# Transposed gating with gates spread by a broadcast load, over lighter query and key DMA, in a fused attention and mixture-of-adapters kernel

## The chip, the cores and the metric

The kernel runs on one core of one Trainium2 chip (trn2). The metric is device time in microseconds (us) of that core, the median of the runs. "Span" is the time from the first to the last instruction of the one profiled execution; a run's time lies about 2 us above its span. A run counts as slow when it lies over 1.5% above the fastest run of the same kernel; comparisons use the others, called fast.

## The reference, cut to what matters

```python
def _attn_ref(q, kv, w_sr):            # q: 4 x 12288 x 128; kv: 4 x 384 x 32 x 128
    kv_pool = kv.reshape(B, H // 4, 4, W // 4, 4, C).mean(axis=(2, 4))
    k = v = kv_pool.reshape(B, -1, C) @ w_sr          # 768 keys a batch
    a = softmax((q @ k.transpose(0, 2, 1)) / sqrt(C))
    return a @ v

def _moe_ref(x, w_gate, A, B):         # x: 49152 x 128; 8 experts of rank 16
    logits = x @ w_gate
    topk = top two experts of each row; w = softmax of their two logits
    delta[row] = sum over the two e of  w_e * ((x[row] @ A[e]) @ B[e])
    return x + delta
```

(The two functions are shortened here to the formulas; `softmax` and `top two` stand for their lines.) The adapters' part, delta, is small beside x. The comparison with the reference doesn't tell right gates from wrong ones.

## The kernel before

The queries are cut into 96 chunks of 512, 24 to a batch; four chunks make a group. The loop is a software pipeline, its instructions kept in program order (`keep`). At step k, TensorE computes the scores of chunk k, the attention sums of an earlier one, and the adapters of still earlier ones.

```python
    def mm(*a, **k):
        return keep(nc.tensor.matmul(*a, **k))        # every matmul has this line: L68
    # ...
    def cast_q(g):                                    # fp32 -> bf16, DRAM to DRAM, issued by GpSimd
        t = qdram.tile([GT, C], BF16, tag=f"q{g}", name=f"qbf{g}")
        keep(nc.gpsimd.dma_start(t, q[g // NG, (g % NG) * GT:(g % NG + 1) * GT]))
        q_bf[g] = t

    def load_qT(g):
        t = qpool.tile([P, GT], BF16, tag="qT", name="qT")
        keep(nc.sync.dma_start(t.rearrange("c (j p) -> c j p", p=P),
                               q_bf[g].rearrange("(p j) c -> p (j c)", p=P), transpose=True))
        qT[g] = t
    # ...
    def scores(k, r):                                 # r = 0, 1, 2: two of six key tiles each
        # ...
        ps = ps_s.tile([P, 2, T], FP32, tag="sg", name="sg")       # two buffers
        for i in range(2):
            mm(ps[:, i], kfT[b][:, 2 * r + i], rhs, start=True, stop=True)
        keep(nc.scalar.activation(em[k][:, 2 * r:2 * r + 2], ps, AF.Exp, bias=0.0, scale=scale))
    # ...
    def gates(k0, n, eng, arg, mask):                 # one call a group, eng is GpSimd
        th = rpool.tile([P, GC * S, 8], FP32, tag="th", name="th")[:, 0:n]
        keep(nc.scalar.activation(th, arg, AF.Tanh, bias=0.0, scale=0.5))
        w = gpool.tile([P, GC * S, 8], FP32, tag="gw", name="gw")
        keep(eng.tensor_tensor(w[:, 0:n], th, mask, op=ALU.mult))
        keep(eng.tensor_tensor(w[:, 0:n], w[:, 0:n], mask, op=ALU.add))
        gw[k0] = w
    # transposes(kx, kh): x of chunk kx and gated h of chunk kh, on TensorE into one PSUM tile
    # of two buffers (tt_ps, pool ps_m), then copied out by VectorE (tts)
    def down(k):
        hp[k] = mtile([P, S, P], name="h_ps")
        for s in range(S):
            mm(hp[k][:, s], xT[k][:, s], a_bf, start=(s == 0), stop=(s == S - 1))

    def gate(k):
        # ...
        keep(nc.vector.tensor_tensor(hg[k] ..., hp[k] ..., gw[k0] ... broadcast over the rank, op=ALU.mult))

    def up(k):
        dp[k] = mtile([P, S, C], name="d_ps")
        for s in range(S):
            mm(dp[k][:, s], hgT[k][:, s], b_bf, start=(s == 0), stop=(s == S - 1))
    # ... when a chunk's x may enter the adapters, in steps:
        done = normed[first[k] + size[k] - 1]         # the group's last chunk is normalized
        late = k < NCHUNK - 2
        # ...
        e = max(e if two else e + 1, done + late)
    # ... in the loop over steps k:
        if k % GC == 0:
            g = k // GC
            if 2 <= g + 1 < B * NG:
                load_qT(g + 1)
            if 4 <= g + 2 < B * NG and g + 2 not in q_bf:
                cast_q(g + 2)
        if b + 1 < B:
            if i == 4:
                sums, rest = prepare(b + 1, nc.gpsimd)    # pooling additions of the next keys
            if 4 <= i < 16:
                h, j = divmod(i - 4, 4)
                load_kv(b + 1, h, j, None)                # 512 KB each
```

The softmax here doesn't subtract the row's maximum and nothing guards it: scores larger than these inputs give would overflow.

## Time and profile before

| | before |
|---|---|
| time, median of 3 fast runs | 426.5 us (426.18 to 426.99) |
| span of the profiled run | 423.3 us |
| start, to the first exp of chunk 4 | 31.5 us |
| chunks 4 to 95, first exp to first exp | 364.2 us |
| tail, after the first exp of chunk 95 | 27.6 us |
| usual period of one chunk | 3.68 us |

The periods are worked out from the trace as the difference between the starts of the first exp of successive chunks.

The page of the kernel before: busy time, share of the span and instruction count of each engine; busy tenths in 40 equal slices for TensorE (PE) and for the DMA engines; DMA packets, MB and share of 16 engines by queue; the chain that ended last, by engine; and three groups of instructions, with busy time, mean nanoseconds of one, and idle time ahead of them with the releaser of most of it.

```profile
span 423.3 us, 11396 instructions
PE 389.1 (92%) x4589; PEld 308.8 (73%) x4589; DVE 327.3 (77%) x967; ACT 292.8 (69%) x336; POOL 162.5 (38%) x263
PE   4898999999999999999999999999999999999853
DMA  8989557776556998765647999998575628342112
q1 hardware_dynamic: 70128, 64.11, 52.7%
q0 software_dynamic: 704, 11.54, 14.5%
PE 72%; DVE 10%; POOL 8%; ACT 3%; DMA 2%; issue 2%; SPq 1%; ACTq 0%; DVEq 0%
...
L246 ACT ACTIVATE em<-sg 128x1024 f16<-128x1024 f32 x288 | 280.5, 1023 | 97.3 <-PE sg L68 96.4
...
L350 DVE TENSOR_TENSOR hg<-h_ps,gw 128x512 bf16<-128x512 f32 x96 | 66.1, 688 | 29.9 <-POOL gw L315 16.1
...
L68 PE MATMUL tt_ps<-id_bf,hg 128*128 128x128 bf16 x384 | 38.1, 223 | 3.2 <-DVE hg L350 2.8
```

TensorE is full in nearly every slice and makes up 72% of the chain; DMA makes up 2%, although its engines are well used (52.7% and 14.5% of the 16 engines' time in the two main queues). The last two groups are what the change is aimed at: VectorE waits 16.1 us for gates that GpSimd (POOL) has late, and 384 matmuls transpose the gated h.

The table of windows of the kernel before, in a stretch without key preparation and over a longer one: the window, its length, busy time of PE, PEld, DVE, ACT and POOL with instruction counts, granted TensorE clock, DMA share, GB/s.

```profile
205.90:238.20 32.30, 32.30 (x407) 26.15 (x406) 27.99 (x79) 24.90 (x28) 8.14 (x17) 1.00 0.72 184
200.00:270.00 70.00, 68.50 (x849) 55.05 (x846) 58.35 (x169) 53.72 (x61) 31.92 (x48) 1.00 0.84 204
```

PE is busy 32.30 of 32.30 us: here only fewer or shorter matmuls make a chunk shorter.

The timeline of the kernel before around one late gate (start, length, engine, line, operation; in brackets the idle time before it and its releaser):

```profile
57.05 0.54 PE L68 MATMUL acc<-vx,em 128*128 128x137 f16 x6
57.42 0.59 PE L68 MATMUL sg<-qT,kfT 128*128 128x512 bf16 x2
...
60.24 2.49 POOL L171 TENSOR_TENSOR kvr<-kvr 128x512 f32<-128x512 f32 x2
...
63.23 0.45 POOL L315 TENSOR_TENSOR gw<-gw,over 128x128 f32<-128x128 f32 x1
63.71 0.69 DVE L350 TENSOR_TENSOR hg<-h_ps,gw 128x512 bf16<-128x512 f32 x1 [1.82 <-POOL gw L315]
```

Two pooling additions hold POOL for 2.49 us, the gates come behind them, and VectorE stands 1.82 us.

### The profile page before, as it was taken

What the parts mean: (1) busy time and instruction counts of PE and PEld (TensorE: products, weight loads), DVE (VectorE), ACT (ScalarE), POOL (GpSimd) and SP (SyncE); (2) the same over time, 40 slices, a digit from 0 to 9 for tenths busy, and PEclk for the clock granted to TensorE, in tenths of its full rate; (3) what the DMA queues carried; (4) which work ended last, traced back from release to release, by engine and by line L of the source; (5) the groups of instructions that cost most, each with busy time, mean ns of one, the idle gap of its engine ahead of it and who ended that gap; (6) DMA issues with size and microseconds to landing.
All of it is one profiled execution on the core that took longest, in us unless ns stands there. A gap on an engine that the chain in (4) does not pass through costs nothing.

```text
span 423.3 us, 11396 instructions
## 1 busy us (share of the span) xinstructions
PE 389.1 (92%) x4589; PEld 308.8 (73%) x4589; DVE 327.3 (77%) x967; ACT 292.8 (69%) x336; POOL 162.5 (38%) x263
## 2 busy tenths in 40 slices
PE   4898999999999999999999999999999999999853
PEld 3566777787877878787888778777888877788642
DVE  2644678788988878779888878779888888888853
ACT  3478567686777777676788777676777866678522
POOL 0010357965320557964330467963231312222000
PEclk9999999999999999999999999999999999999965
DMA  8989557776556998765647999998575628342112
GB/s 302 397 214 284 110 182 199 276 161 140 128 123 134 335 252 258 286 159 114 158 126 150 318 248 164 355 135 182 130 170 129 150 76 175 108 119 75 52 63 88
DMA packets 71172, 76.43 MB, mean 181 GB/s; under 512 B 49904, under 2 KB 50160, under 8 KB 70640
## 3 DMA queue, kind: packets, MB, share of 16 engines
q1 hardware_dynamic: 70128, 64.11, 52.7%
q0 software_dynamic: 704, 11.54, 14.5%
q8 instruction: 36, 0.59, 0.6%
q14 instruction: 16, 0.13, 0.1%
q10 hardware_dynamic: 288, 0.07, 0.1%
HBM read 50.53 MB, written 36.70 MB: 206 GB/s over the span
## 4 chain that ended last, share of the span: by engine, by line
PE 72%; DVE 10%; POOL 8%; ACT 3%; DMA 2%; issue 2%; SPq 1%; ACTq 0%; DVEq 0%
PE acc L68 28%; PE sg L68 23%; PE tt_ps L68 9%; PE d_ps L68 5%; PE h_ps L68 4%; POOL kvr L171 4%; DVE hg L350 3%; ACT em L246 2%; DVE osb L363 2%; DVE xn L263 2%; POOL over L293 1%; PE v_ps L68 1%; SPq L98 1%; PE kpT_ps L68 1%; DMA kvr<-in_kv_dram 1%
## 5 line engine op out<-in xcount | busy, mean ns | idle before, releaser
L246 ACT ACTIVATE em<-sg 128x1024 f16<-128x1024 f32 x288 | 280.5, 1023 | 97.3 <-PE sg L68 96.4
L68 PE MATMUL acc<-vx,em 128*128 128x137 f16 x2304 | 174.1, 224 | 2.0 <-DVE xn L263 1.9
L68 PE MATMUL sg<-qT,kfT 128*128 128x512 bf16 x576 | 170.9, 378 | 2.7 <-ACT em L246 2.2
L68 PEld LDWEIGHTS <-em 128*128 128x128 f16 x2304 | 149.8, 98 | 4.9 <-DVE xn L263 2.2
L68 PEld LDWEIGHTS <-tts 128*128 128x128 bf16 x768 | 59.1, 99 | 53.0 <-ACT tts L334 5.6
L350 DVE TENSOR_TENSOR hg<-h_ps,gw 128x512 bf16<-128x512 f32 x96 | 66.1, 688 | 29.9 <-POOL gw L315 16.1
L293 POOL TENSOR_TENSOR over<-xn,srt 128x128 f32<-128x128 f32 (+1 forms) x54 | 19.8, 384 | 175.7 <-DVE srt L281 175.7
L263 DVE TENSOR_TENSOR xn<-acc,rinv 128x544 f32<-128x544 f32 x96 | 69.5, 724 | 3.3
L171 POOL TENSOR_TENSOR kvr<-kvr 128x512 f32<-128x512 f32 x54 | 67.4, 1268 | 2.1 <-DMA kvr<-in_kv_dram 1.9
L363 DVE TENSOR_TENSOR osb<-d_ps,xn 128x512 f32<-128x512 f32 x96 | 65.9, 689 | 2.7 <-PE d_ps L68 2.6
L336 DVE COPY tts<-tt_ps 128x1024 bf16<-128x1024 bf16 (+1 forms) x95 | 63.9, 672 | 2.4 <-PE tt_ps L68 2.4
L68 PEld LDWEIGHTS <-xn 128*128 128x128 bf16 x384 | 29.5, 99 | 28.6 <-issue 6.1
L68 PEld LDWEIGHTS <-kfT 128*128 128x128 bf16 x576 | 45.9, 97 | 6.0 <-issue 3.7
L68 PE MATMUL h_ps<-a_bf,tts 128*128 128x128 bf16 x384 | 37.6, 221 | 6.1 <-ACT tts L334 3.9
L68 PE MATMUL tt_ps<-id_bf,xn 128*128 128x128 bf16 x384 | 37.5, 221 | 6.0 <-DVE hg L350 4.4
L258 DVE RECIPROCAL rinv<-acc 128x4 f32<-128x4 f32 x96 | 17.3, 180 | 32.9 <-PE acc L68 32.2
L68 PE MATMUL tt_ps<-id_bf,hg 128*128 128x128 bf16 x384 | 38.1, 223 | 3.2 <-DVE hg L350 2.8
L68 PE MATMUL d_ps<-b_bf,tts 128*128 128x128 bf16 x384 | 38.0, 224 | 2.6 <-DVE hg L350 1.0
L281 DVE MAX8 srt<-xn 128x8 f32<-128x8 f32 x384 | 34.5, 153 | 0.2
L68 PEld LDWEIGHTS <-hg 128*128 128x128 bf16 x384 | 26.1, 100 | 4.2 <-DVE hg L350 3.7
L312 ACT ACTIVATE th<-over 128x128 f32<-128x128 f32 (+2 forms) x33 | 9.1, 276 | 15.5 <-DVE over L298 12.2
L314 POOL TENSOR_TENSOR gw<-th,over 128x128 f32<-128x128 f32 (+1 forms) x27 | 11.0, 406 | 21.6 <-ACT th L312 21.5
(49 smaller groups left out, 162.4 us busy)
## 6 DMA issues: line engine op xcount, KB each, us to landing
out_dram<-osb SPq DMA_DIRECT2D x96, 256.0 KB, 3.3
kvr<-in_kv_dram SPq DMA_DIRECT2D x36, 512.0 KB, 6.2
qbf<-in_q_dram POOLq DMA_DIRECT2D x22, 512.0 KB, 6.7
kvr<-in_kv_dram SPq DMA_DIRECT2D x24, 256.0 KB, 4.9
qf<-in_q_dram SPq DMA_DIRECT2D x1, 1024.0 KB, 5.1
qf<-in_q_dram SPq DMA_DIRECT2D x4, 256.0 KB, 5.1
qT<-qbf SPq DMA_TRANSPOSE x22, 8.1
w_sr_sb<-in_w_sr_dram ACTq DMA_DIRECT2D x1, 64.0 KB, 4.7
```

What stands on the lines that cost most here:

```text
L68: return keep(nc.tensor.matmul(*a, **k))
L171: keep(adder.tensor_tensor(u[:, lo:hi], u[:, lo:hi], v[:, lo:hi], op=ALU.add))
L246: keep(nc.scalar.activation(em[k][:, 2 * r:2 * r + 2], ps, AF.Exp, bias=0.0, scale=scale))
L258: keep(nc.vector.reciprocal(ri, acc[k][:, :, VC]))
L263: keep(nc.vector.tensor_tensor(x, acc[k][:, :, 0:VC], ri.unsqueeze(2).broadcast_to([P, S, VC]), op=ALU.mult))
L281: keep(nc.vector.max(srt[k0][:, m, s], xn[k][:, s, C:VC]))
L293: keep(eng.tensor_tensor(d, lg, so[:, :, i].unsqueeze(2).broadcast_to([P, n, 8]), op=ALU.subtract))
L312: keep(nc.scalar.activation(th, arg, AF.Tanh, bias=0.0, scale=0.5))
L314: keep(eng.tensor_tensor(w[:, 0:n], th, mask, op=ALU.mult))
L336: keep(nc.vector.tensor_copy(sb[:, lo:hi], ps[:, lo:hi]))
L350: keep(nc.vector.tensor_tensor(hg[k].rearrange("p s (e r) -> p (s e) r", e=E), hp[k].rearrange("p s (e r) -> p (s e) r", e=E), gw[k0][:, m ...
L363: keep(nc.vector.tensor_tensor(osb, dp[k], xn[k][:, :, 0:C], op=ALU.add))
```

## The change

Intent: for 84 of the 96 chunks, compute h already transposed (one matmul of 512 columns), so that its transpose goes. The gates must then lie along the columns and be the same for the 16 rank rows of an expert. They are transposed once per group on TensorE, written to DRAM (32 KB), and read back 16-fold (512 KB); this trip gets five steps instead of one. Under it, the DMA is rearranged: the query transposes read 16 rows instead of 128 and come two groups ahead, the key loads are cut to 256 KB and spread evenly.

```diff
     def load_qT(g):
         t = qpool.tile([P, GT], BF16, tag="qT", name="qT")
-        keep(nc.sync.dma_start(t.rearrange("c (j p) -> c j p", p=P),
-                               q_bf[g].rearrange("(p j) c -> p (j c)", p=P), transpose=True))
+        keep(nc.sync.dma_start(t.rearrange("c (j r) -> c j r", r=16),
+                               q_bf[g].rearrange("(r j) c -> r (j c)", r=16), transpose=True))
# ... scores: exp now reads PSUM with a step of 64 elements (from group 2 on)
+        if k // GC > 1:
+            ps = ps.rearrange("p i (j s r) -> p i s r j", s=S, r=16)
+            o = o.rearrange("p i (s r j) -> p i s r j", s=S, r=16)
# ... after the tanh of the gates
+        if k0 in turned:                  # chunks 4 to 87: 18 groups of four, 6 of two
+            # ... gh[k0]: the gates in fp16, made on GpSimd
+            turns.append([lambda: turn_gates(k0, n), lambda: spread_gates(k0, n)])
+            return
+    def turn_gates(k0, n):                # one step later
+        ps = mtile([P, P], FP16, name="gT_ps")
+        mm(ps[0:n * E], gh[k0][:, 0:n * E], id_h, is_transpose=True, start=True, stop=True)
+        sb = gtpool.tile([P, P], FP16, tag="gT", name="gT")
+        keep(nc.vector.tensor_copy(sb[0:n * E], ps[0:n * E]))
+        gt[k0] = gdram.tile([P, P], FP16, tag="gt", name="gt")
+        keep(nc.sync.dma_start(gt[k0][0:n * E], sb[0:n * E]))
+
+    def spread_gates(k0, n):              # again one step later
+        gx[k0] = gxpool.tile([P, GT], FP16, tag="gx", name="gx")
+        src = gt[k0][0:n * E].rearrange("(e s) t -> e (s t)", e=E)
+        keep(nc.sync.dma_start(gx[k0][:, 0:n * P],
+                               src.unsqueeze(0).broadcast_to([RK, E, n * P])))
     def down(k):
         hp[k] = mtile([P, S, P], name="h_ps")
+        if first[k] in turned:
+            mm(hp[k], a_bf, xT[k], start=True, stop=True)
+            return
# ... gate: hgT = hp * gx for these chunks; rows of A and B reordered to fit
-        late = k < NCHUNK - 2
+        late = TURN if first[k] in turned else k < NCHUNK - 2      # TURN = 5
# ... other pairs of chunks share a step at the end
+        if k % GC == 0 and 5 <= g + 3 < B * NG:
+            cast_q(g + 3)
+        while nload < min(24 * (B - 1), k + 8, 2 * (k - LA) + 2):   # one 256 KB key load a step
+            bn, n = divmod(nload, 24)
+            load_kv(bn + 1, n // 8, n % 8 // 2, n % 2)
+            nload += 1
+        if k % GC == 1 and 2 <= g + 1 + (g > 1) < B * NG:
+            load_qT(g + 1 + (g > 1))
# ... pools: qpool 4 to 3, ppool 7 to 6, xpool 5 to 6; B loaded in 8 pieces at the start
```

## The prediction

> **What bounds it now.** TensorE. The page gives PE 389.1 of 423.3 us, full granted clock except at the ends. Starts of each chunk's first score matmul, read from the trace: most of 91 periods are 3.68 us; in the stretch 205.9 to 238.2 us the table of windows has PE busy 32.30 of 32.30 us, VectorE 27.99, ScalarE 24.90. That is pure matmul streaming. By the timeline starts lie 0.22 us apart per four 128-column matmuls, 1.12 us per 18 of 137, so: scores about 1.29, attention 1.50, four small groups (x transpose, down, h transpose, up) 0.22 each.
>
> The periods over 3.68 add up to 29 us. About 6 us per later batch are in steps with key preparation. Some 2.7 of these are its own matmuls (timeline); 3.3 are mostly gates late on POOL behind 1.27 us pooling additions (63.2 us: VectorE idle 1.82 us for POOL; the table of waits sums 16.1 us of this). That is about 10 us of the span.
>
> **What the change does.** Of 96 chunks, 84 are gated transposed.
> - PE: the h transpose goes (0.22 us a chunk) and down becomes one 512-column matmul (same time). Added: one 128-column transpose per group, 24 times 0.06. Net -0.22 x 84 + 1.3, about -18 us, all on the critical path; the period becomes about 3.45 us.
> - VectorE: the transpose copy shrinks from 0.69 to 0.42 us (table of groups): about 3.0 us per 3.45.
> - Gates enter the pipeline five steps after normalization instead of one, so lateness on POOL is absorbed: -8 of the 10 us.
> - New DMA chain per group: write gates to DRAM (stores land in 3.3 us), read back 16-fold, 512 KB (loads land in 5 to 6 us). The code leaves some 9.4 us from issue to use, about 1 us of slack: I allow 3 us of waits.
> - Tail: more chunks are unfinished when the scores end (the schedule ends two steps later) (last 24 us: PE busy 10.55). +5 us.
> - Query transposes: 45,056 packets of 256 B, 26 ns each, 74 us of 16 engines; DMA is almost absent from the waits, so lighter or smoother DMA gains little.
> - ScalarE: exp now reads PSUM with a step of 64 elements. Three of 1023 ns per chunk, 2.9 us. [...]this trace has no such read. I take no change. If wrong, ScalarE becomes the bound: at 1.2 us a piece the period is 3.6 and the gain half gone; at twice the time the kernel is far slower.
>
> **Sum.** 423.3 - 18 - 8 + 5 + 3 = 405 us of span; runs lie 2 to 3 us above it: 407 us, 80% range 399 to 420. Faster by over 2% 0.80, within 2% 0.12, slower 0.08.
>
> **What would show it.** Clean periods 3.45 us, PE gapless there; exp mean near 1023 ns; no wait of the gate product for POOL, few for the gate load; steps with key preparation at most 0.6 us over the others; the tail after the last score matmul about 5 us longer; h transposes only for 12 chunks.
>
> **What would make it wrong.** Strided exp slower than 1.15 us; gate loads landing late and blocking VectorE[...]; 16-row query transposes heavier instead of lighter, holding up the SP queue; the tail growing by 10 us or more.

That exp takes no longer with a step of 64 elements was my assumption; no run had shown it then.

## The result, and the profile after

The kernel became slower: 445.75 us, median of 4 runs (444.31 to 449.79), against 426.75 for the kernel before (four runs, one of them slow, 438.66). The ratio is 1.0465, 95% interval 1.0375 to 1.0556. Ratios here are the mean time of one kernel's fast runs over that of the other's of the same rounds, so they are not quite the ratio of the quoted medians.

The page of the kernel after, the same parts, and the DMA issues of the gates (count, KB each, median us from issue to landing):

```profile
span 442.8 us, 10496 instructions
PE 387.9 (88%) x4025; PEld 288.1 (65%) x4025; DVE 308.8 (70%) x987; ACT 297.9 (67%) x341; POOL 163.8 (37%) x263
PE   4897989899989977899899999979999999997464
DMA  8997679999899796878999898899667855433023
q1 hardware_dynamic: 37248, 75.81, 60.5%
q0 software_dynamic: 704, 11.54, 14.8%
PE 48%; DMA 28%; DVE 11%; POOL 5%; issue 3%; ACT 2%; SPq 2%; DVEq 0%; ACTq 0%
...
L256 ACT ACTIVATE em<-sg 128x1024 f16<-128x1024 f32 x288 | 281.6, 1023 | 103.4 <-PE sg L71 102.4
...
L386 DVE TENSOR_TENSOR hgT<-h_ps,gx 128x512 bf16<-128x512 f32 x84 | 58.1, 691 | 35.6 <-DMA gx<-gt 22.6
...
gx<-gt SPq DMA_DIRECT2D x18, 512.0 KB, 5.4
...
gt<-gT SPq DMA_DIRECT2D x18, 32.0 KB, 4.1
```

The 564 matmuls are gone (4,589 to 4,025) and exp costs what it did, 1023 ns, in spite of its step of 64 elements. But PE's row has 7s now, and DMA went from 2% to 28% of the chain. The gate product no longer waits for POOL; it waits 22.6 us for the gates' read-back, gx. (PE's busy time fell by only 1.2 us. A busy PE is not one at full clock: below it is busy 3.00 of 3.00 us at a clock of 0.62. The mean granted clock fell from 0.979 to 0.961; no run splits this number further.) The casts' queue, q0, carries the same 704 packets; the main queue has half the packets, as the query transposes became lighter, but more bytes and a larger share, 60.5% after 52.7%, as the gates' trip came to it.

The timeline of the kernel after, one late read-back link by link:

```profile
162.72 0.58 POOL L82 DMA_DIRECT2D qbf<-in_q_dram  x1
163.22 0.58 SPq L342 DMA_DIRECT2D gt<-gT  x1
...
168.24 0.54 PE L71 MATMUL acc<-vx,em 128*128 128x137 f16 x6
168.70 0.59 PE L71 MATMUL sg<-qT,kfT 128*128 128x512 bf16 x2
...
172.31 0.52 SPq L347 DMA_DIRECT2D gx<-gt  x1
...
177.32 0.69 DVE L386 TENSOR_TENSOR hgT<-h_ps,gx 128x512 bf16<-128x512 f32 x1 [4.38 <-DMA gx<-gt]
...
178.07 0.38 PE L71 MATMUL tt_ps<-id_bf,xn 128*128 128x128 bf16 x4 [3.26 <-DVE hgT L386]
...
179.58 0.38 PE L71 MATMUL d_ps<-b_bf,hgT 128*128 128x128 bf16 x4 [0.53 <-DVE tts L368]
```

A cast of a query group (qbf) leaves at 162.72, the store of the gates (gt) 0.5 us after it. The read-back (gx) needs that store and can't leave before 172.31. It takes its usual 5.0 us, and VectorE stands 4.38 us and PE 3.26 us behind it. VectorE took nothing out of order here: a reciprocal further on in its program (rinv), whose matmuls had ended at 174.37, started at 178.26, after the gate product. Here the store was late, not the load. The table of waits of the kernel after, first by engine (in all, times, longest) and then for SyncE's queue, has the whole run:

```profile
DVE hgT L386 <- DMA gx<-gt: 22.6, 11, 4.4
```

```profile
SPq L347 <- DMA gt<-gT: 41.2, 20, 5.3
```

SyncE must see the store landed before it can send the read-back; it stands 41.2 us in 20 for that. But not all of the eleven waits have a late store. By the landings in the trace, three of them (10.8 of the 22.6 us) came behind a store of over 7 us, two (3.5 us) behind a read-back of over 7 us, and six (8.3 us) behind a store of at most 5.0 and a read-back of at most 6.2 us. In those six the store left late. The timeline of the kernel after ahead of one of them (VectorE's copy of the gates, then SyncE's issues):

```profile
144.21 0.21 DVE L340 COPY gT<-gT_ps 128x128 f16<-128x128 f16 x1
...
144.46 3.54 SPq L410 DMA_DIRECT2D out_dram<-osb  x1
148.05 2.60 SPq L101 DMA_DIRECT2D kvr<-in_kv_dram  x1
150.75 0.54 SPq L342 DMA_DIRECT2D gt<-gT  x1
```

VectorE has written the gates at 144.42. SyncE is then at an output store and a key load, for 3.54 and 2.60 us, and sends the gates behind them, 6.3 us later: it issued in program order and not in the order of what was ready; VectorE waits 2.87 us for them in the end. In the six the store left 1.3 to 6.3 us after the copy.

The chain that ended last, of the kernel after, shows a late store again (start, length, what):

```profile
278.07 7.36 DMA gt<-gT
...
285.49 5.34 DMA gx<-gt
290.93 0.70 DVE hgT L386
```

The 32 KB store takes 7.36 us of the chain and the 512 KB load 5.34.

The table of windows of the kernel after, over the stretch shown of before, in the stall above, and right after it:

```profile
200.00:270.00 70.00, 66.50 (x730) 49.60 (x728) 54.72 (x174) 52.89 (x59) 27.09 (x44) 1.00 0.92 240
...
174.00:181.00 7.00, 3.21 (x27) 2.06 (x25) 3.27 (x11) 2.25 (x3) 6.74 (x8) 0.92 0.92 269
181.00:184.00 3.00, 3.00 (x25) 2.55 (x24) 1.50 (x4) 1.02 (x1) 1.51 (x2) 0.62 1.17 206
```

The DMA share rose from 0.84 to 0.92. In the stall PE is busy 3.21 of 7 us, and in the 3 us after it the granted clock is 0.62. The clock is 0.50 from 179.84 to 183.25 us, after this gap of 3.26 us, and again from 292.5 to 295.9 us, after a gap of 2.63 us. At 180.45 two score matmuls take 1.06 us, at 178.46 and 184.04 they take 0.59. This stall so cost more than its own length: the chunk with it has a period of 9.83 us, where the same chunk without the trip (e3 below) has 4.38.

From the starts of each chunk's first exp, the spans split as follows (us):

| kernel | to the first exp of chunk 9 | chunks 9 to 83 | from chunk 84 to the end | span |
|---|---|---|---|---|
| before | 56.2 | 296.5 | 70.7 | 423.3 |
| after | 58.2 | 299.0 | 85.7 | 442.8 |

So there are two questions. Why did chunks 9 to 83, which lost a matmul group each, not get shorter? And why is the end 15 us longer?

A hint at the first is in the landings. The 24 gate stores took 5.5 us (median) when a cast or a query transpose was in flight for 1.4 us or more of that time, and 3.1 us when for less (at most 0.4 us). The five longest, 6.2 to 9.5 us, all had a cast in flight for 6.0 to 8.4 us of that time. The DMA engines were not busier then (0.72 to 0.92 of the 16 engines) than around the short landings on both sides of 230 us (0.92 to 0.94). A long store has more time to meet a cast, so this alone proves nothing; e11 and e12 test it.

### The profile page after: what moved, and what is told of

It reads as the page before. It is cut to its first block, busy times and chain, and to the rows that moved or that the text cites. A ratio compares the mean times of both kernels' runs of the same rounds, so it can differ in the third digit from the quotient of the medians.

```text
span 442.8 us, 10496 instructions
## 1 busy us (share of the span) xinstructions
PE 387.9 (88%) x4025; PEld 288.1 (65%) x4025; DVE 308.8 (70%) x987; ACT 297.9 (67%) x341; POOL 163.8 (37%) x263
## 3 DMA queue, kind: packets, MB, share of 16 engines
q1 hardware_dynamic: 37248, 75.81, 60.5%
## 4 chain that ended last, share of the span: by engine, by line
PE 48%; DMA 28%; DVE 11%; POOL 5%; issue 3%; ACT 2%; SPq 2%; DVEq 0%; ACTq 0%
PE acc L71 19%; PE sg L71 16%; DMA gx<-gt 9%; DMA gt<-gT 8%; DMA kvr<-in_kv_dram 7%; PE d_ps L71 4%; PE h_ps L71 4%; PE tt_ps L71 4%; POOL kvr L177 2%; DMA a_f<-in_moe_A_dram 2%; DVE hgT L386 2%; DVE tts L368 2%; DVE osb L403 2%; DVE xn L273 2%; ACT tts L366 2%
## 5 line engine op out<-in xcount | busy, mean ns | idle before, releaser
L256 ACT ACTIVATE em<-sg 128x1024 f16<-128x1024 f32 x288 | 281.6, 1023 | 103.4 <-PE sg L71 102.4
L71 PEld LDWEIGHTS <-em 128*128 128x128 f16 x2304 | 153.5, 99 | 21.7 <-DVE xn L273 5.0
L386 DVE TENSOR_TENSOR hgT<-h_ps,gx 128x512 bf16<-128x512 f32 x84 | 58.1, 691 | 35.6 <-DMA gx<-gt 22.6
L71 PEld LDWEIGHTS <-kfT 128*128 128x128 bf16 x576 | 48.1, 98 | 16.9 <-issue 9.8
L71 PEld LDWEIGHTS <-hgT 128*128 128x128 bf16 x336 | 25.6, 98 | 30.0 <-issue 13.4
L268 DVE RECIPROCAL rinv<-acc 128x4 f32<-128x4 f32 x96 | 17.4, 181 | 37.2 <-PE acc L71 37.1
L368 DVE COPY tts<-tt_ps 128x512 bf16<-128x512 bf16 (+1 forms) x90 | 38.2, 424 | 2.0 <-PE tt_ps L71 2.0
L71 PE MATMUL d_ps<-b_bf,hgT 128*128 128x128 bf16 x336 | 32.3, 220 | 7.5 <-DVE tts L368 7.1
L71 PE MATMUL h_ps<-tts,a_bf 128*128 128x512 bf16 x84 | 32.2, 384 | 2.5 <-DVE tts L368 2.5
L323 ACT ACTIVATE th<-over 128x128 f32<-128x128 f32 (+2 forms) x33 | 9.0, 274 | 14.4 <-DVE over L309 11.0
L175 POOL TENSOR_TENSOR kvr<-kvr 128x512 f32<-128x512 f32 (+1 forms) x18 | 18.0, 998 | 1.4
L71 PEld LDWEIGHTS <-tts 128*128 128x128 bf16 x96 | 8.1, 118 | 15.0 <-ACT tts L366 11.8
L366 ACT COPY tts<-tt_ps 128x1024 bf16<-128x1024 bf16 (+1 forms) x10 | 8.0, 796 | 14.7 <-PE tt_ps L71 14.7
```

The costliest lines, as they stand in the source:

```text
L175: keep(adder.tensor_tensor(u, u, v, op=ALU.add))
L256: keep(nc.scalar.activation(o, ps, AF.Exp, bias=0.0, scale=scale))
L268: keep(nc.vector.reciprocal(ri, acc[k][:, :, VC]))
L366: keep(nc.scalar.copy(sb[:, lo:hi], ps[:, lo:hi]))
L368: keep(nc.vector.tensor_copy(sb[:, lo:hi], ps[:, lo:hi]))
L386: keep(nc.vector.tensor_tensor(hgT[k], hp[k], gx[k0][:, m * T:(m + 1) * T].rearrange("p (s t) -> p s t", s=S), op=ALU.mult))
```

## The experiments

The quoted expectations name some theories by letters and say there what each means; the text around them uses words. The table gives each kernel's time, and the same three stretches of its profiled run. Slow runs are in the medians and ranges and not in the ratios, so the ratios of e2, e15 and e16 rest on two fast runs each. One run of the kernel before took 668.27 us, at a clock of 0.562; it counts as slow.

| run | median (range), us | before | ratio of fast runs, 95% interval | to chunk 9 | 9 to 83 | 84 to end |
|---|---|---|---|---|---|---|
| e1 | 426.55 (426.14–427.21) | 426.71 | 1.0001 [0.9982, 1.0020] | 56.3 | 296.6 | 71.4 |
| e2 | 451.75 (444.85–455.28) | 426.71 | 1.0471 [1.0408, 1.0533] | profile of a slow run | | |
| e3 | 425.35 (425.16–425.59) | 426.71 | 0.9971 [0.9956, 0.9987] | 58.8 | 279.4 | 85.5 |
| e4 | 434.94 (433.79–438.75) | 426.71 | 1.0224 [1.0161, 1.0287] | 59.4 | 288.3 | 84.1 |
| e5 | 434.9 (433.84–436.44) | 426.57 | 1.0190 [1.0158, 1.0222] | 59.0 | 288.0 | 87.7 |
| e6 | 451.99 (448.25–466.53) | 426.57 | 1.0558 [1.0509, 1.0607] | 60.9 | 302.2 | 87.1 |
| e7 | 438.37 (435.40–440.17) | 426.57 | 1.0261 [1.0211, 1.0312] | 58.1 | 294.0 | 83.2 |
| e8 | 431.86 (431.31–433.95) | 426.57 | 1.0125 [1.0090, 1.0161] | 58.5 | 283.8 | 88.0 |
| e9 | 429.85 (425.16–435.82) | 426.66 | 1.0075 [1.0048, 1.0102] | 58.2 | 279.4 | 85.7 |
| e10 | 440.15 (436.43–444.12) | 426.66 | 1.0287 [1.0233, 1.0341] | 59.4 | 294.5 | 85.4 |
| e11 | 425.68 (424.99–427.92) | 426.66 | 0.9986 [0.9954, 1.0018] | 59.3 | 279.3 | 84.3 |
| e12 | 434.06 (431.94–435.35) | 426.66 | 1.0169 [1.0132, 1.0205] | 59.2 | 286.2 | 85.6 |
| e13 | 427.48 (421.90–432.41) | 426.91 | 0.9955 [0.9916, 0.9994] | profile of a slow run | | |
| e14 | 426.86 (422.43–433.03) | 426.91 | 0.9955 [0.9916, 0.9994] | profile of a slow run | | |
| e15 | 436.61 (431.98–444.64) | 426.91 | 1.0135 [1.0115, 1.0156] | 60.7 | 286.0 | 84.3 |
| e16 | 442.80 (434.44–448.08) | 427.02 | 1.0213 [1.0124, 1.0302] | 63.6 | 282.7 | 86.4 |
| e17 | 460.34 (458.77–461.50) | 427.02 | 1.0759 [1.0706, 1.0812] | 63.5 | 308.9 | 85.9 |
| e18 | 421.02 (419.38–421.78) | 426.10 | 0.9865 [0.9826, 0.9903] | 57.8 | 276.3 | 84.6 |

### e1_dma_only and e2_gating_only: the two halves apart

e1 is the kernel before with the DMA half alone: 16-row query transposes two groups ahead, the strided exp and the permuted store that follow from them, and 256 KB key loads at one pace. e2 is the kernel after with that half undone. Neither changes the other half's lines.

```diff
 # e1, against the kernel before
+        keep(nc.sync.dma_start(t.rearrange("c (j r) -> c j r", r=16), ..., transpose=True))
+            ps = ps.rearrange("p i (j s r) -> p i s r j", s=S, r=16)      # in scores
+        while nload < min(24 * (B - 1), k + 8, 2 * (k - LA) + 2): ...     # key loads
+        if k % GC == 1 ...: load_qT(g + 1 + (g > 1))
```

> Only the DMA half of the change (16-row query transposes two groups ahead, the permuted exp and store, key loads of 256 KB at one pace), with the old gating. Theory W (the loss in the main part is the new gates' trip through DRAM arriving late at VectorE): no gate load here, so about the time before, 418 to 428 us. Rival D (the new pattern of DMA is itself the loss): 435 us or more, with waits for keys or queries.

> Only the gating half, over the old DMA (128-row transposes one group ahead, key loads in bursts of 512 KB). Theory W: the gate loads are as late or later, so 440 to 460 us, with the gate product waiting 20 us or more for the gate load. Rival D: 405 to 420 us, since the DMA pattern is gone.

The DMA half alone changed nothing: ratio 1.0001, and each stretch within 0.7 us of the kernel before. The gating half alone carried the whole loss, 1.0471 against 1.0465 for both. (Its profile is of a slow run, so it is no measure; the gate product waits 33.4 us for the read-back in it.) The query transposes did get lighter: by the packets in the trace, 45,056 of 256 B, 74.3 us of 16 engines' time, became 352 of 32 KB, 52.1 us. Their median landings were 8.1 us in the kernel before and 6.6 in the kernel after, counted from where SyncE reaches the instruction, so with its waits for a free buffer. That relief was on nothing that ended a wait.

### e3_no_gate_dma and e4_traffic_no_wait: the trip's wait, or its traffic

Both multiply h by a constant, so no instruction waits for the read-back (the result is wrong). e4 still sends both DMAs; e3 sends neither.

```diff
 # e4, against the kernel after
+    gconst = const.tile([P, T], FP16)
+    nc.vector.memset(gconst, 0.5)
-                hgT[k], hp[k], gx[k0][:, m * T:(m + 1) * T].rearrange("p (s t) -> p s t", s=S),
+                hgT[k], hp[k], gconst.rearrange("p (s t) -> p s t", s=S),
 # e3, in addition
-        keep(nc.sync.dma_start(gt[k0][0:n * E], sb[0:n * E]))
-        keep(nc.sync.dma_start(gx[k0][:, 0:n * P], ...))
```

> The changed kernel with constant gates and neither gate DMA; wrong result on purpose. Theory W: the 22.6 us of waits of the gate product and what follows them go, the tail of 39 us stays: 412 to 421 us. Rival D: over 432 us. The clean period tells of a third point: if it stays at 3.53 us instead of the 3.45 us of the matmuls, it is not the gate load that holds it up but the score buffer waiting for the exp.

> The changed kernel with both gate DMAs kept, in the same queue and at the same places, but the gate product reads a constant; wrong result on purpose. If the loss is the wait of VectorE for the gates (W): like e3, within 4 us of it. If it is what the added traffic and the blocked SP queue do to the other transfers (rival C): within 6 us of the changed kernel, 436 us or more.

Without the trip (e3) chunks 9 to 83 take 279.4 us, not 299.0. The trip costs 19.6 us there, and without it the new matmul order is 17.1 us shorter than the kernel before. The total still came to 425.35 us and missed what I expected. The end is as long as in the kernel after (85.5 us). The first exp of chunk 4 came 2.2 us later than there, as my memset on VectorE moved the order of the first instructions; 0.6 us of that is left at chunk 9.

e4 fell between the two theories: the waits are gone, yet it is 8.9 us longer than e3 in chunks 9 to 83. One period of 11.89 us, 4.38 in e3, is most of that. The timeline of e4 there:

```profile
275.33 1.27 POOL L177 TENSOR_TENSOR kvr<-kvr 128x512 f32<-128x512 f32 x1 [2.71 <-DMA kvr<-in_kv_dram]
279.21 1.26 POOL L177 TENSOR_TENSOR kvr<-kvr 128x512 f32<-128x512 f32 x1 [2.62 <-DMA kvr<-in_kv_dram]
...
280.96 0.73 POOL L327 TENSOR_TENSOR gh<-th,over 128x128 f16<-128x128 f32 x1
...
281.74 0.10 PEld L71 LDWEIGHTS <-gh 128*128 128x128 f16 x1 [5.15 <-POOL gh L327]
```

Two key loads landed late and held POOL's pooling additions, 2.71 and 2.62 us; the gates stood behind the additions on POOL (their tanh on ScalarE had ended at 273.54, POOL took it up at 280.43), and PE stood 5.15 us for them. So the traffic alone can also cost, through POOL, though it did so once. SyncE was far behind by then: in this stretch gate stores left up to 17.0 us after VectorE had written the gates.

### e5_turn6 and e7_short_turned: more slack, and the end

e7 turns only chunks 4 to 71, so that the old gating, with its lag of one step, runs the end. e5 does the same and gives the trip six steps. (A lag of seven deadlocks when the program is built, so it has no run.)

```diff
 # e7
-    turned = {... 4 <= k0 < NCHUNK - 8}
+    turned = {... 4 <= k0 < NCHUNK - 24}
 # e5, in addition
-    TURN = 5
+    TURN = 6
```

> Gates enter six steps after normalization instead of five, so each gate load has one step, 3.5 us, more; transposed gating ends 16 chunks earlier, as in the third run of this set, so that the buffers suffice. If lateness of the gate loads is the loss in the main part (W): the 22.6 us of waits of the gate product for the gate load fall under 8 us, and the time is 8 us or more below the third run's. If the wait only moves (rival Q: the issue in the SP queue slides with the backlog, whatever the slack): still over 15 us of waits, within 4 us of the third run.

> Transposed gating ends at chunk 72 instead of 88, so the lag of five steps is caught up while scores still run. Theory T (the tail grew because the lag leaves more chunks when the scores end): from the last chunk's first score matmul to the end 28 to 31 us as in the kernel before, against 39.4 us, of which about 3 us come back as 16 chunks more with the long gating: 434 to 440 us in all. Rival: the tail stays at 36 us or more, because the last chunks are slow for another reason, such as the backlog of stores.

e7's tail, after the first exp of chunk 95, fell to 28.8 us from 38.7, as expected, but chunks 84 to 94 rose from 46.9 to 54.4 us. That is the catching up. Chunks that entered with a lag of five must be finished two in a step before the lag can be one. From chunk 84 on e7 takes 83.2 us, the kernel after 85.7, the kernel before 70.7. So the end costs 12 to 15 us wherever it is paid. That the lag is the reason fits e5, where one step more costs 4.5 us more, but no run has the new gating with a short lag.

In e5 the read-back waits fell to 7.3 us in 2 from 17.4 us in 9 (e7), below the 8 expected, and chunks 9 to 83 fell from 294.0 to 288.0 us. But the gain of the total over e7 was 3.5 us and not 8, as the longer lag gave part of it back at the end (87.7 against 83.2).

### e6_own_ring: is it SyncE's queue?

The gate store waits in a queue that also carries key loads, outputs and query transposes. e6 issues both gate DMAs from ScalarE.

```diff
-        keep(nc.sync.dma_start(gt[k0][0:n * E], sb[0:n * E]))
+        sends.append(lambda: keep(nc.scalar.dma_start(gt[k0][0:n * E], sb[0:n * E])))
-        keep(nc.sync.dma_start(gx[k0][:, 0:n * P], ...
+        keep(nc.scalar.dma_start(gx[k0][:, 0:n * P], ...
 # the sends are issued behind exp of a step, to keep exp first
```

> Both gate transfers issued from ScalarE's queue, placed after an exp that has long been issued, so that they neither stand behind key loads, stores and query transposes in SP's queue nor hold SP up; nothing else moves. If queueing behind the bulk transfers of the same queue makes the gates late (theory F): the store of gates lands in under 3 us in the median instead of 4.1 with a longest of 9.5, the waits for the gate load fall under 6 us, 424 to 432 us in all. If the 16 engines are simply full (rival C): landings and waits as before, 440 us or more.

The total missed by far, but the run is not a clean test. The DMA issues of e6, to be set beside the 4.1 and 5.4 us of the kernel after:

```profile
gt<-gT ACTq DMA_DIRECT2D x18, 32.0 KB, 3.6
gx<-gt ACTq DMA_DIRECT2D x18, 512.0 KB, 7.5
```

The store lands a little sooner (the longest takes 6.4 us, not 9.5) and the read-back later (the longest 12.8, not 9.3). The waits for the read-back fell from 22.6 to 11.9 us, where under 6 was expected. But exp on ScalarE now waited for DMA, 10.0 us in 6 by the table of waits, and PE waited 14.4 us for exp where the kernel after waits 2.2, and the total is 451.99 us. So SyncE's queue has a part in the waits, not all of them, and this way around it cost more than it gave.

### e8_order_no_gate_dma and e9_order_lag_tail: the periods without a stall

Even e3, without any trip, has a usual period of 3.53 us where I expected 3.45, and 3.89 in every fourth step. Two details in the kernel after's timeline above suggest why. In the clean step the six attention matmuls start at 168.24 and the next scores 0.46 us later, where they followed after 0.37 before; ScalarE is then still in the exp that frees one of the two score buffers (the first of three that start at 167.62, 1.02 us each). And the gate transpose takes one of the two PSUM buffers (pool ps_m) every fourth step, which shifts the rotation so that the `up` matmuls wait for VectorE's copy (0.53 us at 179.58).

The edit moves one attention group ahead of the last scores, and puts the gates' transpose into the unused half of tt_ps. e8 does this on e3, e9 on the kernel after with lag six and chunks turned to 71.

```diff
             attend(ka[0], 0)
+            attend(ka[0], 1)
             # scores(k, 2) follows
-            for s in range(1 if len(ka) == 1 else 0, S):
+            for s in range(2 if len(ka) == 1 else 0, S):
 # gate transpose: no tile of its own
-        ps = mtile([P, P], FP16, name="gT_ps")
+        ps = spare.pop()[:, 1, 0].bitcast(FP16) if spare else mtile([P, P], FP16, name="gT_ps")
```

(e8; in e9 the gate transpose is issued before the copy out of tt_ps instead of after it, and the store behind that copy.)

> The kernel with constant gates (425.35 us; wrong result on purpose), with two edits on TensorE: half of the attention instead of a quarter stands before the third score group, and the gate transpose writes into the unused half of the x transpose's PSUM tile instead of a tile of its own. Theory S (the clean period of 3.53 us instead of 3.45 is the third score group waiting for the exp that frees its buffer; the 3.89 us of each fourth step is the PSUM tile of the gate transpose shifting the two-buffer rotation): clean period 3.44 to 3.47, fourth steps 3.50 to 3.55, 411 to 417 us. Rival: periods stay, so VectorE or ScalarE sets them.

> A correct kernel from what is known so far: lag of six steps, transposed gating to chunk 72, half of the attention before the third score group, and the gate transpose placed in the x transpose's PSUM tile before the copy out of it, so that it waits for no copy. Theory S: clean period 3.45 us and each fourth step 3.5 us instead of 3.89; tail as in e5 (36.6 us) or less. 416 to 426 us, beside 434.9 us of e5. If S is wrong about the fourth steps they stay at 3.8 us or more.

The clean period became 3.45 us in both, as expected. In e8 the fourth steps got worse, 4.37 us, and the total missed. The table of waits of e8 shows that this was my edit's own:

```profile
PE tt_ps L71 <- DVE tts L365: 16.9, 22, 1.3
```

The gate transpose wrote into the tile that VectorE was still copying out. In e9, where it is issued before that copy, the fourth steps take 3.50 us, so the theory of the shifted buffers holds. Chunks 9 to 83 took 279.4 us in e9's profiled run, with two stalls left, periods of 7.80 and 7.52 us, both in steps with key preparation. That run is its fastest; the runs spread from 425 to 436 us, and the median of 429.85 missed the 416 to 426 expected.

### e10_small_casts, e11_no_casts and e12_later_casts: does the cast hold the store up?

e10 reshapes the cast in the hope of smaller packets. e11 leaves the casts out of the loop and reads an old group (wrong). e12 keeps them and issues them two steps later in each group.

```diff
 # e10
-        keep(nc.gpsimd.dma_start(t, q[...]))
+        keep(nc.gpsimd.dma_start(t.rearrange("(p j) c -> p (j c)", p=P), src.rearrange("(p j) c -> p (j c)", p=P)))
 # e11
-            cast_q(g + 3)
+            q_bf[g + 3] = q_bf[2]
 # e12
-        if k % GC == 0 and 5 <= g + 3 < B * NG:
+        if k % GC == 2 and 5 <= g + 3 < B * NG:
```

> The changed kernel with the casting transfers of the queries (DRAM to DRAM) cut into 128 rows, so that their packets are of some 4 KB instead of 32 KB (about 3 us each); same bytes, same places. In the changed kernel the store of gates took a median of 5.5 us with a cast or query transpose in flight and 3.1 us without. Theory P (a small transfer waits behind 32 KB packets on each engine): stores of gates land in under 4 us also beside casts, the longest under 6 us; the waits for the gate load fall under 10 us from 22.6; 428 to 438 us. Rival C (the 16 engines are too full, whatever the size of a packet): landings and time as before, 442 us or more.

> The changed kernel without the casts after group 4 (later groups read group 2's queries; wrong result on purpose): 20 of the 22 casts' traffic, about 55 of 336 us of the 16 engines, goes. Theory P and rival C both: waits for the gate load under 6 us, the longest landing of a store of gates under 5 us, 420 to 430 us (421 us would be the constant-gates run less its slower start). If the waits stay over 15 us, the casts are not what delays the gates, and key loads or transposes are.

> The changed kernel with each cast issued two steps later, away from the store and the load of gates; same packets, same bytes. Theory P, and any theory that it is the meeting with a cast that delays the gates: longest landing of a store of gates under 6 us, waits for the gate load under 10 us, 428 to 438 us. Rival C (fullness): no change, 442 us or more.

e10 settles nothing on packets: the casts' stayed 352 of 32 KB. It is in effect a repeat of the kernel after: 440.15 us instead of 445.75, 294.5 us instead of 299.0 for chunks 9 to 83, and 19.5 us of waits for the read-back in 12. So a difference of that size between calls is no evidence. e11 settles most. (It drops 19 of the 22 casts, not the 20 expected.) No instruction waits for a read-back, the longest gate store takes 4.1 us, and chunks 9 to 83 take 279.3 us, the same as without the trip (279.4 in e3). SyncE keeps up, too: 23 of the 24 stores left within 0.03 us of VectorE's copy, where in the kernel after 16 left over 1 us late. The 32 KB store takes 1.5 us in the median and the 512 KB load 5.3, where the kernel after has 4.1 and 5.4. In e11 the trip costs nothing. e12 keeps every transfer and only moves it. Its line in the table of waits:

```profile
DVE hgT L386 <- DMA gx<-gt: 3.0, 4, 2.3
```

3.0 us instead of 22.6; the longest store takes 5.2 us, not 9.5. Chunks 9 to 83 take 286.2 us. So it is the meeting of the cast and the trip that costs, not the amount of transfers. Of the 19.6 us, e12 takes back 12.8 (8.3 if e10 is taken as the kernel after). The rest is in steps with key preparation, longer in e12 than in e3 (4.7 to 5.3 us against 4.1 to 4.4, and one of 6.1). At least part of it comes with the moved cast itself, as e9 and e14 show below.

### e15_split_casts: is it the size of the cast's packets?

```diff
-        keep(nc.gpsimd.dma_start(t, q[...]))
+        for j in range(0, 16, 8):
+            keep(nc.gpsimd.dma_start(dst[:, j:j + 8], src[:, j:j + 8]))
```

> The changed kernel with each cast as two transfers of half rows that can't be merged, so that the profile should show packets of 2 to 4 KB in the software queue instead of 352 of 32 KB; same bytes, same places. Theory P (small transfers wait behind 32 KB packets): longest landing of a store of gates under 6 us instead of 9.5, waits for the gate load under 10 us, 428 to 437 us. If it is the cast's traffic itself, whatever its packets: landings of 7 us and more remain, 438 us or more.

The page of e15 shows the split took effect, in the line of the software queue (packets, MB, share):

```profile
q0 software_dynamic: 6336, 11.54, 18.0%
```

The same bytes went in 6,336 packets instead of 704; the casts' own are 5,632 of 2 KB instead of 352 of 32 KB. The waits for the read-back fell from 22.6 to 10.5 us in 9, where I expected under 10, and the longest store from 9.5 to 7.3, where I expected under 6. That a store waits behind the cast's 32 KB packets, 3.0 us each in the mean in the kernel after, was my theory. In this profile half of the waits left with the large packets and half stayed. But it is of one of the two faster runs (432.89 us); the others took 440.33 and 444.64, as long as the kernel after or e10. So packet size may be a part, and that is not shown.

### e13_all_lag5 and e14_all_lag6: the best version that I could form

Later casts, the new matmul order, the gate transpose in the unused half tile, chunks turned to 71; lag five (e13) or six (e14).

> A correct kernel with every term found so far undone: casts two steps later, transposed gating to chunk 72, half of the attention before the third score group, gate transpose in the x transpose's PSUM tile before the copy; lag of five steps as in the change. If the terms account for the loss: clean period 3.45 us, waits for the gate load under 5 us, from the last chunk's first exp to the end 29 us (e7), 411 to 421 us in all, faster than the kernel before by 1 to 4%. If something is still missing: 424 us or more.

> The same with a lag of six steps. If the waits for gates are gone at five steps already, a sixth buys nothing and costs a longer tail (e5: 35.8 us against 28.8 of e7): 3 to 7 us more than e13. If e13 still has gate waits of over 8 us, this one is the faster.

Both missed. By their fast runs they are 0.45% faster than the kernel before, but by the medians (427.48 and 426.86 against 426.91) they are equal to it, and they spread from 421.9 to 433 us where it keeps within 1.4 us. Both profiled runs were slow ones. In e13's, one period was 13.99 us: a read-back took 9.4 us to land with a cast in flight for 8.3 us of it. The cast had left in its planned step; the gates were late. A query transpose held SyncE for 8.34 us, 7.32 of them for a buffer that PE had yet to free, and the gate store left 7.6 us after VectorE's copy. So the place of a transfer in the program doesn't hold it at a place in time: SyncE runs behind, and POOL issues casts up to 2.8 us into their step behind its additions.

The move of the casts has a price of its own. e14 and e9 differ in nothing else. PE waits 7.8 us in 8 for the gates of POOL (gh) in e14 and 2.9 us in 7 in e9, and steps with pooling additions that take 4.5 us in e9 take 5.1 in e14, as in e18 below, whose run was fast. POOL's issue of the cast, 0.58 us, stands right before its last two instructions for the gates there.

### e16_casts_after_gates and e17_turn_step_later: tying the cast to the gates

In e16 POOL first reads one column of the landed read-back and only then issues the next cast, two steps into a group. In e17 the cast is moved one step on, and the gate transpose as well.

```diff
 # e16, against e14
-        if k % GC == 2 and 5 <= g + 3 < B * NG: ...        # at the start of the step
+        if k % GC == 2 and 6 <= g + 4 < B * NG:
+            if k - 10 in gx:
+                keep(nc.gpsimd.tensor_copy(landed, gx[k - 10][:, 0:1]))
+            cast_q(g + 4)
 # e17: 3 and 11 in place of 2 and 10, and
-        waiting += turns
+        waiting += ready
+        ready[:] = turns
```

> e14 (lag six; 426.86 us median, 422.43 to 433.03) with each cast held on POOL until that round's gate load has landed, one group further ahead. If meetings with casts are what is left: waits for the gate load under 2 us, no chunk period over 6.7 us after chunk 9, and runs that agree within 1%: 417 to 424 us. If gate waits of over 6 us remain without a cast in flight, key loads, stores and transposes are enough to make the gates late.

> e16 with the gate transpose, the store and the load of gates one step later (so a slack as at a lag of five). Waits of TensorE for gates from POOL fall from some 20 us to under 4 us, and each fourth period in the stretches with key preparation from 5.1 to about 4.4 us: 3 to 6 us below e16 if the gate load still comes in time; above e16 if it does not.

Both missed. In e16 no cast was in flight during a read-back and none took over 7.1 us, so the tie works. VectorE still waited 9.8 us in 6, behind stores of at most 4.3 us: a cast in flight is not needed for a stall. And the table of waits has POOL standing for it:

```profile
POOL landed L517 <- DMA gx<-gt: 44.1, 16, 4.8
```

The additions and the next gates are behind that wait, and four casts at the start (the tie needs one more group ahead) made it 5.4 us longer than the kernel after's. e17 left the trip too few steps: VectorE waited 43.9 us in 14. All read-backs landed within 6.3 us; six of the 17 stores took 6.5 to 8.8, but ten of the waits (32.3 us) came behind stores of at most 5.1. So a late store is not needed for a stall; the slack is small by itself.

### e18_all_no_trip: what the rest is worth

e13 with constant gates and no trip (wrong, the constant set by GpSimd so that the start stays as it was).

> e13 with constant gates and neither gate transfer (wrong result on purpose). If the trip is all that is left: clean period 3.45 us, no period over 6.7 us, runs that agree within 0.5%, from the last chunk's first exp to the end 29 us, 408 to 414 us in all, which is the size of gain that the prediction had. If 418 us or more, the transposed gating as scheduled loses elsewhere too.

421.02 us, ratio 0.9865, and all six runs within 0.6% of each other. So the spread of e13 and e14 comes with the trip. The time is above the 408 to 414 us expected: even a free trip would gain 1.35% with this schedule. Chunks 9 to 83 take 276.3 us, 20.2 less than before; from chunk 84 on it is 84.6 us, 13.9 more. In chunks 9 to 83 a wait took the old one's place, by e18's table of waits:

```profile
PEld L71 <- POOL gh L327: 11.0, 9, 2.1
...
PE tt_ps L71 <- POOL gh L327: 7.5, 8, 1.2
```

The weight load and its matmul wait for the same gates, so the two are not to be added. The gates are still late on POOL behind the additions and the moved cast, and now it is PE's transpose of them that waits. It comes two steps after normalization, whatever the lag, so the five steps don't cover it. The nine such steps are 0.57 to 0.62 us shorter in e9, which leaves the casts in place, 5.4 us in all; so e18 is not the most that a free trip could give.

## Why the prediction was wrong, point by point

I predicted 407 us (399 to 420) and the kernel takes 445.75. In spans, predicted 405 and measured 442.8, 37.8 us apart. The stretches above show where, in spans:

| term of the sum | predicted | measured | difference |
|---|---|---|---|
| trip of the gates, "I allow 3 us of waits" | +3 | +19.6 (after less e3, chunks 9 to 83) | 16.6 |
| the rest of chunks 9 to 83 | −24, estimated as 75/84 of −18, and −8 | −17.1 (e3 less before) | 6.9 |
| end, from chunk 84 | +3, estimated as "+5" less 2 of matmuls | +15.0 | 12 |
| start, to chunk 9 | 0 | +2.0 | 2 |

- **The step that failed first is "The code leaves some 9.4 us from issue to use, about 1 us of slack: I allow 3 us of waits."** I took landings of 3.3 and 5 to 6 us from the kernel before and treated them as fixed. The trip is two landings in a row, which took up to 9.5 and 9.3 us beside a cast, and its store left up to 6.3 us late from SyncE's queue. Taking the casts away (e11) or the trip (e3) gives the same 279 us for chunks 9 to 83, and moving the casts (e12) takes 22.6 us of waits to 3.0. I had named "gate loads landing late and blocking VectorE" as what could make it wrong; that is what happened, by late stores, late read-backs and late issues (10.8, 3.5 and 8.3 of the 22.6 us).
- **"Tail: … +5 us" was mis-sized.** From chunk 84 on it is +15.0 us; after the first exp of chunk 95 alone it is +11.1. Chunks with a lag of five steps are still to be finished then, and e7 and e18 show that the cost only moves when they are caught up earlier (83.2 and 84.6 us, against 70.7 before). That all of it is the lag's is argued, not shown.
- **"The period becomes about 3.45 us" failed by 0.08 us, and by 0.4 in every fourth step.** I added matmul times and left out the order: two score buffers and two small PSUM buffers. In e9 a different order gave 3.45 and 3.50 us, so the sum of matmuls was right and the term for buffers was missing.
- **"Gates enter the pipeline five steps after normalization instead of one, so lateness on POOL is absorbed" was half right.** VectorE no longer waits for POOL, and e3's steps with key preparation take at most 4.38 us where the kernel before has 5.42. But PE's gate transpose now waits for POOL in them (1.8 us in all in the kernel after, more in e4 and e18).
- **The start** was not in the sum. The period of chunk 5 is 5.09 us instead of 3.31, with VectorE waiting 7.5 us for the load of A behind eight small loads of B. Only the profile shows this; no run tested it alone.
- **Right:** exp with a step of 64 elements is unchanged at 1023 ns; the h transposes are gone for 84 chunks; VectorE's copy takes 0.42 us; the DMA half is worth nothing by itself (e1).

Still open is how a cast delays the trip. That casts do is shown (e11, e12). SyncE's queue has a part in it (stores that leave up to 6.3 us late; waits of 11.9 us instead of 22.6 in e6), but what of the lateness is landing and what is queueing no run separates. The engines' busy share was no higher in the long landings (0.72 to 0.92 against 0.92 to 0.94). Packet size may be part of it (e15). Nor did I find out what makes single runs of e13 and e14 as fast as 422 us and others 433, beyond that it comes with the trip (e18).

## What to carry to other kernels

A round trip through DRAM in a pipeline is two latencies in a row (here 4.1 and 5.4 us in the median, up to 9.5 and 9.3). Its slack must be set by the longest landing beside the other traffic of the kernel, not by the median of a quieter one, and by when the queue that issues it gets there (here up to 6.3 us late). When a trace shows which transfers are in flight at the late ones, try to move those (e12 took 434.06 us, moving the trip to another queue 451.99), and look at what now stands behind them on their own engine. A longer lag is paid at the end as unfinished work (one step more cost 4.5 us there, e5 against e7), and that bill belongs into the sum before the gain per chunk is counted. Where TensorE is full, a removed matmul shortens the period only if the buffers it rotated through still come free in time: redo the order of the remaining work, not only the sum (the period was 3.53 us in e3 and 3.45 in e8, after the reordering).
